# Attention and two feed-forward layers on one core: the token blocks cut as 4 x 512 + 256 instead of 512 + 4 x 448, with new planner constants

## The chip, the cores and the metric

The kernel runs on one core of a Trainium2 chip. The metric is the time of one execution in device microseconds (us); the time of a kernel is the median of its runs.

## The reference

Three steps, in float32, on 4 sequences of 576 tokens (2304 tokens in all) with 8 heads of 64:

```python
scores = q @ k.T / 8            # heads 0-3: keys at distance 0..31 back
                                # heads 4-7: keys at the same position modulo 32, not ahead
attn = softmax(scores) @ v      # -> x, 2304 x 512
xn = x / sqrt(mean(x*x) + 1e-6) * rms_g
y1 = (silu(xn @ w_gate) * (xn @ w_val)) @ w_out      # 512 -> 1536 -> 512
out = relu(y1 @ w_in)**2 @ w_out2                    # 512 -> 2048 -> 512
```

Nearly all of the arithmetic is in the two feed-forward layers: 2304 tokens through five matrices.

## The kernel before

**Attention.** There are 16 units: 4 sequences times 4 pairs of heads (two pairs of each mask). For a unit SyncE loads q, k and v, PE makes the scores, DVE takes the maximum, ACT the exponentials (`att_exp`, L414) and PE multiplies with v (`att_pv`, L502); ACT writes the result to `xr` (L536). In the first `NM2` units the mask is added by two matmuls (L354), in the others by DVE (L380).

**Feed-forward.** The tokens are cut into the blocks of the table `BLOCKS` (L49). Each layer is done in two halves of its hidden width, which makes four phases (`PHASES`): 6 + 6 tiles `j` of 128 hidden columns in layer 1, 8 + 8 in layer 2. A phase goes over the five blocks, and in a block over its tiles. So one tile of one block, a *slot*, is `ff_in` (12 matmuls, or 24 in layer 1 with gate and value) and `ff_out` (12). A matmul product is made of three passes, L1114 to L1116 (high x high, high x low, low x high parts of the operands in float32r), each with its own 128x128 weight load; a pass streams as many columns as the block has tokens, 512 or 448. On PE the order is in(j), out(j-1), in(j+1), out(j). Behind `ff_in`, `after_in` takes the sums out of PSUM: ACT makes tanh or relu (L1165, L1181), DVE gates or squares (L1169, L1177, L1185), rounds to the high part (L1194) and subtracts for the low part (L1199). Sums of `ff_out` are taken out at the end of a block (L1286, L1290, L1292).

**Weights.** They arrive as 64-bit numbers, in pairs of 128x512 tiles, and `w_task` turns each pair into high and low float32r parts: ACT or DVE takes the magnitude (L1040, L1042), DVE guards (L1049) and shifts (L1052, L1058, L1063), ACT or DVE rounds (L1072, L1074), DVE or POOL subtracts twice (L1080). The pairs live in rings of 9 and, after attention, 4 more; a pair's place comes free when the last block of its phase has used it (`through`). So the pairs of the next phase that have no place yet are made during the last block of this one.

**Norm.** `prep_task` sums the squares of runs of at most 128 tokens on PE (`chunks`, `prep_ms`), takes the inverse root on POOL, spreads it over the partitions (`prep_bc`), and DVE scales `xr` (L816). `split_tasks` makes the high part on ACT (L831) and the low part on DVE or POOL (L839).

**What sets the order.** A planner in Python walks through the program while it is built. It holds a clock for each engine, a list of tasks with due times (in slots) and a cost for each step (`dve`, `act`, `gps`, and constants such as `MXP`, `LOADF`, `TOL`), and emits the next instruction of the engine that can start first. Each engine then runs its list strictly in that order. While the planner sees PE idle before the first feed-forward matmul it puts in small matmuls on zeros (L1359). All DMAs of loads and stores stand in one list, that of SyncE (SP).

Of the kernel before, what the change touches and what calls it, by code (L numbers as in the profile page):

```python
# [16 lines left out]
B, H, S, D = 4, 8, 576, 64  # L17
# [28 lines left out]
QL, KL = {"loc": QW["loc"], "str": SL}, {"loc": KW["loc"], "str": SL}  # L46
QKW = max(QL[t] + KL[t] for t in ("loc", "str"))

BLOCKS = [(0, 512), (512, 448), (960, 448), (1408, 448), (1856, 448)]  # L49
NMAX = 512  # L50
CH = 128
NB = len(BLOCKS)
# [1 line left out]

RING, RING2 = 9, 4

ATT_LEAD, ATT_STEP = 6, 0.032
PREP_LEAD = 7.755
W_LEAD = 0.5
X_LEAD = 4.644  # L60
WARM0 = 20

HOP = 0.15
DRAIN = 0.12
TOL = 0.135
FILL, FILL_OF, T0, W1_AT = 0.113, 0.8, 5.3, 6.041
NRAW = 2
EXP = 2
QKB, SMB, TRB, PTB = 2, 3, 2, 2

NM2 = 8
QK0, PV0 = {"loc": 1.0, "str": 0.9}, {"loc": 1.25, "str": 0.9}

PRI = {"qk": -1, "mask": 1, "mx": -3, "exp": -3, "eps": -3, "sum": -1, "norm": 2, "turn": 0, "keep": 4, "tr": -3,
       "swap": 0, "pv": 9, "out": 20, "sq": 20, "ms0": 0, "add": -4}
MXP, LOADF, BIAS = 2, 0.926, 0.5

# [21 lines left out]
def chunks(i):  # L99

    out = []
    for b, s0, m in segments(*BLOCKS[i]):
        k = -(-m // CH)
        out += [(b, s0 + m - CH * (k - e)) for e in range(k)]
    return out


# [41 lines left out]
def dvx(n, fast=False):  # L149
    return [("X", (60 + n / (2 if fast else 1)) / 960 + 0.1)]  # L150


def act(n, psum=False):
    return [("A", ((172 if psum else 224) + n) / 1200 + 0.02)]


def gps(n):
    return [("P", n / 420 + 0.1)]


@with_exitstack
def kernel(ctx: ExitStack, tc: tile.TileContext, loc, strd, w1, w2, g, cst, out):
# [34 lines left out]
    ident = cst_sb[:, 0:128].bitcast(F32)  # L197
# [103 lines left out]
    first_acc, warming, ms0 = [], [True], []  # L301
# [244 lines left out]
    def att_ms0(u):  # L546

        t = ssq[0] if u == 0 else sm_t[u]
        for e, (_, s0) in enumerate(chunks(0)):
            nc.tensor.matmul(  # L550
                out=ms0[0][:CH, e:e + 1], lhsT=t[:, s0:s0 + CH], rhs=ones, start=False,
                stop=u == NPAIR - 1 and e == len(chunks(0)) - 1,
            )
# [10 lines left out]
    def att_task(u, due):  # L564
        b, p = units[u]
        kd = kind(u)
# [39 lines left out]
        def exp(i0, i1):  # L606
            def f(_, t):
                att_exp(u, i0, i1)
                if NM <= u < NM2:
                    for h in range(2):  # L610
                        if i0 < nt * (h + 1) <= i1:
                            give("s", t)
            return (None, [[("A", 0.3 * (i1 - i0) + 0.02)]], f, None, due - PRI["exp"])

        def norm(parts, t):
            att_norm(u, nc.gpsimd if parts[0][0] == "P" else nc.vector)
# [128 lines left out]
        ))  # L745
        for a in range(2):
            steps.append(step(
                "out", None, [[("A", 0.45 if kd == "loc" else 0.63)]], outp(a),
                (lambda: rel["xr"][0]) if p + a == 0 else None,
            ))  # L750
        steps.append(step(
# [5 lines left out]
        if not alone:  # L757
            m = S - add_from(b)
# [10 lines left out]
    def prep_ms(i):  # L769
        if i == 0:  # L770
            pend[0] = ms0[0], st_p.tile([128, 8], F32, tag="inv", name="inv")
            return
        ps = s_p.tile([128, 512], F32, tag="s", name="msb")
        inv = st_p.tile([128, 8], F32, tag="inv", name="inv")
        for e, (b, s0) in enumerate(chunks(i)):
            nc.tensor.matmul(out=ps[:CH, e:e + 1], lhsT=ssq[b][:, s0:s0 + CH], rhs=ones, start=True, stop=True)  # L776
        pend[i] = ps, inv

# [26 lines left out]

    def xn_parts(i, k):
# [13 lines left out]
    def split_tasks(key, due, n, src, before=None, after=None):  # L820

        cell = {"n": 0}

        def hi(k):
            def f(_, t):
                if "t" not in cell:
                    cell["t"] = x_p.tile([128, 2, KDM, NMAX], F32R, tag="x", name="xt")
                    take("x")
                    turn("x")
                for o, x in src(k):  # L830
                    nc.scalar.activation(out=cell["t"][:, 0, k, o:o + x.shape[-1]], in_=x, func=ACTF.Copy)  # L831
# [21 lines left out]
        out = []  # L853
        for k in range(KDM):
            steps = [(room_x, [act(n)], hi(k), x_time), (None, [dvx(n), gps(n)], lo(k), None)]
            out.append(Task(due, ([] if before is None else [before(k)]) + steps))
        return out

    def prep_task(i, due):
# [39 lines left out]
        def xn(k):  # L899
# [122 lines left out]
    def w_task(n, due):  # L1022
# [47 lines left out]
        def hi(parts, t):  # L1070
            if parts[0][0] == "A":
                nc.scalar.activation(out=cell["w"][:, :, 0], in_=cell["r"], func=ACTF.Copy)  # L1072
            else:
                nc.vector.tensor_copy(cell["w"][:, :, 0], cell["r"])  # L1074

        def lo(e):
            def f(parts, t):
# [397 lines left out]
```

## Time and profile before

| | |
|---|---|
| median of 3 runs | 943.73 us (940.89 to 945.85) |
| the profiled execution | 943.36 us |
| its span, first to last instruction | 941.4 us, mean granted TensorE clock 0.995 |
| PE busy, weight loads busy | 98%, 88% |
| DVE, ACT, POOL busy | 61%, 30%, 4% |
| first feed-forward matmul, last one | 50.76 us, 936.70 us after the span's start |

How to read it: the span is the profiled execution's, and some 2 us lie around it. A busy PE is not a PE at its peak, because matmuls overlap; how fast it really goes is read from the distance of the starts of its matmuls. Line numbers Lnnn are of the kernel before; the change adds two lines ahead of most of them.

### The profile page before, as it was taken

How to read it: one execution, taken by the hardware profiler on the slowest of the kernel's cores; microseconds unless marked ns; L12 is line 12 of the kernel's file. 1: busy time of each engine (PE TensorE's matmuls, PEld its weight loads, DVE VectorE, ACT ScalarE, POOL GpSimd, SP SyncE). 2: the span in 40 equal slices, each digit the busy share in tenths (PEclk: the TensorE clock that was granted, in tenths of full speed). 3: DMA queues.
4: the chain of work that ended last, by engine and by line, in shares of the span. 5: the costliest groups of instructions: out<-in, count | busy, mean ns of one | idle time of the engine just before them, and what ended most of it. 6: DMA issues, size and time to landing. Idle time of an engine off the chain costs nothing.

```text
span 941.4 us, 15656 instructions
## 1 busy us (share of the span) xinstructions
PE 927.3 (98%) x6525; PEld 829.5 (88%) x6525; DVE 576.2 (61%) x941; ACT 285.4 (30%) x773; POOL 41.0 (4%) x42
## 2 busy tenths in 40 slices
PE   8999999999999999999999999999999999999998
PEld 6777888899999888999999988999999889999997
DVE  5898856556969884243438999344459535435343
ACT  5976755523233411011112323121122211111110
POOL 0133401010000000000000000000000000000000
PEclk9999999999999999999999999999999999999999
DMA  9755654314534533030303434230221203122011
GB/s 339 236 206 182 224 170 123 113 65 183 181 132 152 178 134 123 1 118 1 123 1 128 159 138 164 99 118 1 84 76 48 79 1 123 32 87 78 1 40 39
DMA packets 47365, 105.40 MB, mean 112 GB/s; under 512 B 4160, under 2 KB 31296, under 8 KB 46272
## 3 DMA queue, kind: packets, MB, share of 16 engines
q1 hardware_dynamic: 47296, 104.41, 32.8%
q8 instruction: 51, 0.84, 0.4%
q14 instruction: 18, 0.15, 0.0%
HBM read 77.20 MB, written 23.59 MB: 107 GB/s over the span
## 4 chain that ended last, share of the span: by engine, by line
PE 94%; DMA 3%; ACT 1%; DVE 1%; issue 0%; POOL 0%; SPq 0%; DVEq 0%
PE gv L1114 18%; PE gv L1115 18%; PE gv L1116 18%; PE a L1114 12%; PE a L1115 12%; PE a L1116 12%; DMA qk<-in_loc 2%; PE xo L502 1%; PE sc L366 1%; PE a L457 1%; DMA qk<-in_strd 1%; ACT sm L414 1%; PE bc L799 0%; DMA v<-in_strd 0%; PE msb L776 0%
## 5 line engine op out<-in xcount | busy, mean ns | idle before, releaser
L1114 PE MATMUL gv<-xt,w 128*128 128x448 f32 (+1 forms) x800 | 299.2, 374 | 0.0
L1115 PE MATMUL gv<-xt,w 128*128 128x448 f32 (+1 forms) x800 | 297.0, 371 | 0.0
L1116 PE MATMUL gv<-xt,w 128*128 128x448 f32 (+1 forms) x800 | 296.8, 371 | 0.0
L1114 PE MATMUL a<-hd,w 128*128 128x448 f32 (+1 forms) x560 | 207.9, 371 | 0.0
L1115 PE MATMUL a<-hd,w 128*128 128x448 f32 (+1 forms) x560 | 207.3, 370 | 0.0
L1116 PE MATMUL a<-hd,w 128*128 128x448 f32 (+1 forms) x560 | 207.2, 370 | 0.0
L1114 PEld LDWEIGHTS gv<-xt,w 128*128 128x128 f32 x800 | 150.6, 188 | 16.6
L1115 PEld LDWEIGHTS gv<-xt,w 128*128 128x128 f32 x800 | 150.7, 188 | 16.2 <-POOL xt L839 0.4
L1116 PEld LDWEIGHTS gv<-xt,w 128*128 128x128 f32 x800 | 150.7, 188 | 15.9
L1185 DVE TENSOR_TENSOR t<-t,gv 128x448 f32<-128x448 f32 (+1 forms) x80 | 50.7, 634 | 175.9 <-ACT t L1181 175.8
L1181 ACT ACTIVATE t<-gv 128x448 f32<-128x448 f32 (+1 forms) x80 | 44.4, 555 | 303.2 <-PE gv L1116 303.1
L1114 PEld LDWEIGHTS a<-hd,w 128*128 128x128 f32 x560 | 105.2, 188 | 11.2
L1115 PEld LDWEIGHTS a<-hd,w 128*128 128x128 f32 x560 | 105.2, 188 | 11.1 <-DVE hd L1199 0.2
L1116 PEld LDWEIGHTS a<-hd,w 128*128 128x128 f32 x560 | 105.2, 188 | 11.0
L1165 ACT ACTIVATE t<-gv 128x448 f32<-128x448 f32 (+1 forms) x60 | 33.2, 553 | 209.6 <-PE gv L1116 209.4
L1169 DVE SCALAR_TENSOR_TENSOR t<-t,gv 128x448 f32<-128x448 f32 (+1 forms) x60 | 37.9, 632 | 85.0 <-ACT t L1165 84.9
L1199 DVE TENSOR_TENSOR hd<-t,hd 128x448 fp32r<-128x448 f32 (+1 forms) x136 | 86.8, 639 | 4.8 <-ACT hd L1192 0.3
L1177 DVE TENSOR_TENSOR t<-t,gv 128x448 f32<-128x448 f32 (+1 forms) x60 | 37.9, 632 | 40.5 <-PE gv L1116 39.9
L1194 DVE CAST hd<-t 128x448 fp32r<-128x448 f32 (+1 forms) x132 | 52.8, 400 | 9.3
L1040 ACT ACTIVATE raw<-wst 128x1024 f32<-128x1024 f32 x24 | 27.3, 1142 | 40.6 <-DMA wst<-in_w 33.3
L414 ACT ACTIVATE sm<-sm,nm 128x64 f32<-128x64 f32 x88 | 29.3, 335 | 17.6 <-DVE nm L402 17.5
L839 DVE TENSOR_TENSOR xt<-xs,xt 128x448 fp32r<-128x448 f32 (+1 forms) x60 | 34.3, 632 | 0.0
(86 smaller groups left out, 673.2 us busy)
## 6 DMA issues: line engine op xcount, KB each, us to landing
wst<-in_w SPq DMA_DIRECT2D x34, 1024.0 KB, 5.0
yp_d<-ys SPq DMA_DIRECT2D x8, 896.0 KB, 4.3
ypt<-yp_d SPq DMA_DIRECT2D x8, 896.0 KB, 7.9
xs<-y_d SPq DMA_DIRECT2D x8, 896.0 KB, 5.1
qk<-in_strd SPq DMA_DIRECT2D x8, 604.0 KB, 6.4
qk<-in_loc SPq DMA_DIRECT2D x8, 592.0 KB, 6.0
xs<-xn_d SPq DMA_DIRECT2D x4, 896.0 KB, 5.5
y_d<-ys SPq DMA_DIRECT2D x4, 896.0 KB, 4.8
```

The lines of the kernel that those rows point to most:

```text
L414: nc.scalar.activation(out=sm[:, i], in_=sm[:, i] if sc is None else sc[h][:, 64 * t:64 * t + 64], func=ACTF.Exp, bias=nm[:, i:i + 1], sca ...
L839: eng.tensor_tensor(out=cell["t"][:, 1, k, c], in0=x, in1=cell["t"][:, 0, k, c].bitcast(F32), op=ALU.subtract)
L1114: nc.tensor.matmul(out=o, lhsT=whi, rhs=x_hi, start=first, stop=False)
L1115: nc.tensor.matmul(out=o, lhsT=whi, rhs=x_lo, start=False, stop=False)
L1116: nc.tensor.matmul(out=o, lhsT=wlo, rhs=x_hi, start=False, stop=last)
L1165: nc.scalar.activation(out=tile_t()[:, :n], in_=ps[:, :n], func=ACTF.Tanh, scale=0.5)
L1169: nc.vector.scalar_tensor_tensor(out=t_sb[:, :n], in0=t_sb[:, :n], scalar=1.0, in1=ps[:, :n], op0=ALU.add, op1=ALU.mult)
L1177: nc.vector.tensor_tensor(out=t_sb[:, :n], in0=t_sb[:, :n], in1=ps[:, :n], op=ALU.mult)
L1181: nc.scalar.activation(out=tile_t()[:, :n], in_=ps[:, :n], func=ACTF.Relu)
L1185: nc.vector.tensor_tensor(out=t_sb[:, :n], in0=t_sb[:, :n], in1=ps[:, :n], op=ALU.mult)
L1194: nc.vector.tensor_copy(hid[key][0][:, 0, :n], tmps[key][:, :n])
L1199: eng.tensor_tensor(out=hd[:, 1, :n], in0=t_sb[:, :n], in1=hd[:, 0, :n].bitcast(F32), op=ALU.subtract)
```

## The change

`BLOCKS` becomes four blocks of 512 tokens and a last one of 256. The number of slots and of matmuls in the feed-forward layers stays as it is. Because block ends now fall at other places of the sequences, `chunks` names for each run its first token in the sequence, how many of 128 to skip, and its length, and `prep_bc` uses these. The planner gets other leads, priorities and costs, and the masks of a ninth unit are added by PE.

```diff
-BLOCKS = [(0, 512), (512, 448), (960, 448), (1408, 448), (1856, 448)]
+BLOCKS = [(0, 512), (512, 512), (1024, 512), (1536, 512), (2048, 256)]
...
-ATT_LEAD, ATT_STEP = 6, 0.032
-PREP_LEAD = 7.755
-W_LEAD = 0.5
-X_LEAD = 4.644
+ATT_LEAD, ATT_STEP = 7, 0
+PREP_LEAD = 2.463
+W_LEAD = 2.25
+X_LEAD = 3.773
...
-TOL = 0.135
-FILL, FILL_OF, T0, W1_AT = 0.113, 0.8, 5.3, 6.041
+TOL = 0.215
+FILL, FILL_OF, T0, W1_AT = 0.113, 0.8, 5.3, 9.414
...
-NM2 = 8
+NM2 = 9
...
-MXP, LOADF, BIAS = 2, 0.926, 0.5
+MXP, LOADF, BIAS = 16, 0, 0.729
-PV_AHEAD = 3
+PV_AHEAD = 2
...
     for b, s0, m in segments(*BLOCKS[i]):
-        k = -(-m // CH)
-        out += [(b, s0 + m - CH * (k - e)) for e in range(k)]
+        for o in range(0, m, CH):
+            c = min(CH, m - o)
+            first = min(s0 + o, S - CH)
+            out.append((b, first, s0 + o - first, c))
...
 def gps(n):
-    return [("P", n / 420 + 0.1)]
+    return [("P", n / 400 + 0.18)]
...
-        for e, (b, s0) in enumerate(chunks(i)):
-            skip = CH * len(chunks(i)) - BLOCKS[i][1] if e == 0 else 0
+        for e, (_, _, skip, m) in enumerate(chunks(i)):
             nc.tensor.matmul(
-                out=ps[:, o:o + CH - skip], lhsT=inv[:CH, e:e + 1].to_broadcast([CH, 128]), rhs=ident[:CH, skip:CH],
+                out=ps[:, o:o + m], lhsT=inv[:CH, e:e + 1].to_broadcast([CH, 128]), rhs=ident[:CH, skip:skip + m],
                 start=True, stop=True,
             )
-            o += CH - skip
+            o += m
```

Left out: the table `PRI` of priorities (nearly every entry is another) and five costs of ACT and PE steps.

**What moves: SyncE's list at the start.** The sixth to tenth transfers of the program (`wst` is a pair of raw weights, `qk` and `v` are a unit's inputs). Before:

```order
L329 DMA v<-in_strd 128x768
L996 DMA wst<-in_w 128x2x1024
L321 DMA qk<-in_loc 128x1184
L323 DMA qk<-in_strd 128x2x604
L996 DMA wst<-in_w 128x2x1024
```

With the change:

```order
L331 DMA v<-in_strd 128x768
L323 DMA qk<-in_loc 128x1184
L325 DMA qk<-in_strd 128x2x604
L998 DMA wst<-in_w 128x2x1024 x2
L323 DMA qk<-in_loc 128x1184
```

The second pair of weights now stands behind the q and k of units 2 and 3, and directly ahead of the third pair.

**DVE ahead of the first feed-forward matmul.** (`xr` is the attention output, `xt` the block's split operand, `w` a pair's split parts.) Before:

```order
L428 RECIPROCAL ri<-su 128x10
L435 TENSOR_TENSOR sm<-sm,ri 128x640
L1063 SCALAR_TENSOR_TENSOR raws<-wst,raws 128x1024
L816 SCALAR_TENSOR_TENSOR xr<-xr,g_sb,bc 128x512 x4
L839 TENSOR_TENSOR xt<-xr,xt 128x512 x3
```

With the change:

```order
L430 RECIPROCAL ri<-su 128x10
L437 TENSOR_TENSOR sm<-sm,ri 128x640
L1076 CAST w<-raws 128x2x512
L817 SCALAR_TENSOR_TENSOR xr<-xr,g_sb,bc 128x512 x4
L840 TENSOR_TENSOR xt<-xr,xt 128x512 x4
```

All four low parts of the first block are now DVE's; one of them was POOL's. In this list up to the low parts there are one rounding and one subtraction of weights more than before.

**DVE in the last block of phase 0, its first two slots.** Before (448 tokens):

```order
L1169 SCALAR_TENSOR_TENSOR t<-t,gv 128x448
L1177 TENSOR_TENSOR t<-t,gv 128x448
L1194 CAST hd<-t 128x448
L1199 TENSOR_TENSOR hd<-t,hd 128x448
L1049 TENSOR_SCALAR raw<-raw 128x1024
L1052 TENSOR_SCALAR raw<-raw 128x1024
L1292 TENSOR_SCALAR ys<-a_3313 128x448
L1058 SCALAR_TENSOR_TENSOR raw<-wst,raw 128x1024
L1063 SCALAR_TENSOR_TENSOR raw<-wst,raw 128x1024
L1169 SCALAR_TENSOR_TENSOR t<-t,gv 128x448
```

With the change (256 tokens):

```order
L1171 SCALAR_TENSOR_TENSOR t<-t,gv 128x256
L1179 TENSOR_TENSOR t<-t,gv 128x256
L1196 CAST hd<-t 128x256
L1201 TENSOR_TENSOR hd<-t,hd 128x256
L1051 TENSOR_SCALAR raw<-raw 128x1024
L1054 TENSOR_SCALAR raw<-raw 128x1024
L1060 SCALAR_TENSOR_TENSOR raw<-wst,raw 128x1024
L1294 TENSOR_SCALAR ys<-a_3333 128x512
L1065 SCALAR_TENSOR_TENSOR raw<-wst,raw 128x1024
L1171 SCALAR_TENSOR_TENSOR t<-t,gv 128x256
```

The same operations stand there; those of the block are 256 wide, those of the weights as wide as before. From the first gate (L1171) of this block to its last low part (L1201) the list holds, beside the block's own operations, three each of L1051, L1054, L1060 and L1065, four of L1082 (subtraction of weights) and one eviction (L1294).

## Rows read from the trace of the kernel before

**Rows 1.** The page, busy time by engine.
```profile
PE 927.3 (98%) x6525; PEld 829.5 (88%) x6525; DVE 576.2 (61%) x941; ACT 285.4 (30%) x773; POOL 41.0 (4%) x42
```
**Rows 2.** Groups of instructions by line: busy us, mean ns of one | idle before.
```profile
L1114 PE MATMUL gv<-xt,w 128*128 128x448 f32 (+1 forms) x800 | 299.2, 374 | 0.0
...
L1114 PE MATMUL a<-hd,w 128*128 128x448 f32 (+1 forms) x560 | 207.9, 371 | 0.0
...
L1114 PEld LDWEIGHTS gv<-xt,w 128*128 128x128 f32 x800 | 150.6, 188 | 16.6
```
**Rows 3.** Stretches: length, busy PE PEld DVE ACT POOL, granted clock, DMA share, GB/s.
```profile
50.70:115.30 64.60, 64.07 (x829) 51.35 (x819) 56.11 (x83) 46.98 (x176) 24.10 (x22) 1.00 0.61 206
115.30:176.70 61.40, 59.49 (x838) 52.12 (x837) 36.87 (x69) 36.93 (x156) 3.68 (x4) 0.97 0.45 134
...
270.30:314.40 44.10, 44.10 (x218) 40.60 (x217) 38.82 (x57) 17.18 (x23) 0.00 (x0) 1.00 0.42 138
314.40:362.80 48.40, 48.40 (x218) 40.53 (x217) 39.56 (x58) 13.33 (x19) 0.00 (x0) 1.00 0.42 147
```
**Rows 4.** Timeline of PE, a block of 512: starts of two slots four slots apart.
```profile
322.44 0.39 PE L1114 MATMUL gv<-xt,w 128*128 128x512 f32 x1
...
355.08 0.39 PE L1114 MATMUL gv<-xt,w 128*128 128x512 f32 x1
```
**Rows 5.** The same, a block of 448.
```profile
414.34 0.36 PE L1114 MATMUL gv<-xt,w 128*128 128x448 f32 x1
...
443.52 0.36 PE L1114 MATMUL gv<-xt,w 128*128 128x448 f32 x1
```
**Rows 6.** Timeline of PE: eight loads with one column each; zeros of 256 columns, two windows.
```profile
98.02 0.95 PE L776 MATMUL msb<-ones,ssq 128*128 128x1 f32 x8
...
8.19 3.54 PE L1359 MATMUL warm<-blank 128*128 128x256 bf16 x30
...
8.19 2.98 PE L1359 MATMUL warm<-blank 128*128 128x256 bf16 x25
```
**Rows 7.** Groups by form: DVE and ACT operations of a block.
```profile
L1199 DVE TENSOR_TENSOR hd<-t,hd 128x448 fp32r<-128x448 f32 x110 | 68.8, 626 | 4.0 <-ACT hd L1192 0.3
L1194 DVE CAST hd<-t 128x448 fp32r<-128x448 f32 x110 | 43.4, 394 | 7.6
L1169 DVE SCALAR_TENSOR_TENSOR t<-t,gv 128x448 f32<-128x448 f32 x48 | 29.7, 619 | 79.0 <-ACT t L1165 79.0
L1199 DVE TENSOR_TENSOR hd<-t,hd 128x512 fp32r<-128x512 f32 x26 | 18.0, 692 | 0.8
...
L1181 ACT ACTIVATE t<-gv 128x448 f32<-128x448 f32 x64 | 34.8, 544 | 245.4 <-PE gv L1116 245.3
```
**Rows 8.** Groups by form: DVE operations of a pair of weights.
```profile
L1080 DVE TENSOR_TENSOR w<-raw,w 128x512 fp32r<-128x512 f32 x49 | 32.1, 686 | 1.3 <-ACT w L1072 1.0
L1058 DVE SCALAR_TENSOR_TENSOR raw<-wst,raw 128x1024 int32<-128x1024 int32 x25 | 30.6, 1223 | 0.5
```
**Rows 9.** Timeline, the start: when unit 2 and the second weights came.
```profile
16.52 1.13 ACT L1040 ACTIVATE raws<-wst 128x1024 f32<-128x1024 f32 x1 [0.34 <-DMA wst<-in_w]
...
18.06 0.71 PE L366 MATMUL a<-qk 64*32 64x64 f32 x46 [0.92 <-DMA qk<-in_loc]
...
20.20 0.82 DVE L397 TENSOR_REDUCE nm<-a 128x10 f32<-128x640 f32 x1 [1.38 <-PE a L366]
```
**Rows 10.** Timeline, the first feed-forward matmuls and the low parts they wait for.
```profile
49.27 4.23 DVE L839 TENSOR_TENSOR xt<-xr,xt 128x512 fp32r<-128x512 f32 x3
...
51.30 0.19 PEld L1115 LDWEIGHTS gv<-xt,w 128*128 128x128 f32 x1 [0.35 <-POOL xt L839]
```
**Rows 11.** Timeline of PE, the longest wait in phase 0 and matmuls behind it.
```profile
145.91 1.04 PE L502 MATMUL xo<-pt,v 64*64 64x64 f32 x44 [1.91 <-DMA v<-in_strd]
...
147.69 0.58 PE L1114 MATMUL gv<-xt,w 128*128 128x448 f32 x1
...
150.31 0.58 PE L1115 MATMUL gv<-xt,w 128*128 128x448 f32 x1
```

More of the change, by code (lines that the diff above doesn't have):

```diff
@@ L69 @@
 QKB, SMB, TRB, PTB = 2, 3, 2, 2
-NM2 = 8
+NM2 = 9
 QK0, PV0 = {"loc": 1.0, "str": 0.9}, {"loc": 1.25, "str": 0.9}
-PRI = {"qk": -1, "mask": 1, "mx": -3, "exp": -3, "eps": -3, "sum": -1, "norm": 2, "turn": 0, "keep": 4, "tr": -3,
-       "swap": 0, "pv": 9, "out": 20, "sq": 20, "ms0": 0, "add": -4}
-MXP, LOADF, BIAS = 2, 0.926, 0.5
-D_BUSY, D_COST = 120, 1.1
-PV_AHEAD = 3
+PRI = {"qk": 1, "mask": 0, "mx": -1, "exp": 0, "eps": 0, "sum": 0, "norm": 2, "turn": -5, "keep": 0, "tr": 0,
+       "swap": -1, "pv": 0, "out": 0, "sq": -3, "ms0": -3, "add": -3}
+MXP, LOADF, BIAS = 16, 0, 0.729
+D_BUSY, D_COST = 121.519, 1.1
+PV_AHEAD = 2
 NM = 6
@@ L548, in att_ms0 @@
         t = ssq[0] if u == 0 else sm_t[u]
-        for e, (_, s0) in enumerate(chunks(0)):
+        for e, (_, s0, _, _) in enumerate(chunks(0)):
             nc.tensor.matmul(
@@ L612, in f @@
                             give("s", t)
-            return (None, [[("A", 0.3 * (i1 - i0) + 0.02)]], f, None, due - PRI["exp"])
+            return (None, [[("A", 0.33 * (i1 - i0))]], f, None, due - PRI["exp"])
         def norm(parts, t):
@@ L747, in att_task @@
             steps.append(step(
-                "out", None, [[("A", 0.45 if kd == "loc" else 0.63)]], outp(a),
+                "out", None, [[("A", 0.47 if kd == "loc" else 0.73)]], outp(a),
                 (lambda: rel["xr"][0]) if p + a == 0 else None,
@@ L774, in prep_ms @@
         inv = st_p.tile([128, 8], F32, tag="inv", name="inv")
-        for e, (b, s0) in enumerate(chunks(i)):
+        for e, (b, s0, _, _) in enumerate(chunks(i)):
             nc.tensor.matmul(out=ps[:CH, e:e + 1], lhsT=ssq[b][:, s0:s0 + CH], rhs=ones, start=True, stop=True)
@@ L796, in prep_bc @@
         o = 0
-        for e, (b, s0) in enumerate(chunks(i)):
-            skip = CH * len(chunks(i)) - BLOCKS[i][1] if e == 0 else 0
+        for e, (_, _, skip, m) in enumerate(chunks(i)):
             nc.tensor.matmul(
-                out=ps[:, o:o + CH - skip], lhsT=inv[:CH, e:e + 1].to_broadcast([CH, 128]), rhs=ident[:CH, skip:CH],
+                out=ps[:, o:o + m], lhsT=inv[:CH, e:e + 1].to_broadcast([CH, 128]), rhs=ident[:CH, skip:skip + m],
                 start=True, stop=True,
             )
-            o += CH - skip
+            o += m
         pend[i] = ps, inv
@@ L853, in split_tasks @@
         out = []
+        two = 0.23 * (len(list(src(0))) - 1)
         for k in range(KDM):
-            steps = [(room_x, [act(n)], hi(k), x_time), (None, [dvx(n), gps(n)], lo(k), None)]
+            steps = [(room_x, [[("A", act(n)[0][1] + two)]], hi(k), x_time), (None, [dvx(n), gps(n)], lo(k), None)]
             out.append(Task(due, ([] if before is None else [before(k)]) + steps))
@@ L927, in prep_task @@
             (None, [[("P", 1.1)]], pw, None),
-            (lambda: room("s"), [[("T", 0.4 * nch)]], bc, lambda: rel["s"][0]),
+            (lambda: room("s"), [[("T", 0.25 * nch)]], bc, lambda: rel["s"][0]),
         ]))
@@ L1089, in w_task @@
                 and (keys[0][0] == 0 or "raw" in late),
-                [dvx(1024, fast=True), act(1024)], size,
+                [dvx(1024, fast=True), [("A", 1.14)]], size,
                 lambda: max(
```

## The prediction

> **What bounds the kernel now.** I read the page first: PE is busy for 98% of the span, no other engine for two thirds [rows 1]. A busy PE may still be a slow one, so the next view is the timeline of PE, for the distance between the starts of its matmuls. In a block of 512 tokens two slots that are four slots apart start at 322.44 and 355.08 us [rows 4]. A slot of layer 1 has 36 matmuls, so 32.64 us / 144 = 226.7 ns each. In a block of 448 it is 29.18 us / 144 = 202.6 ns [rows 5]. The granted clock is 1.00 there, the level of 2.4 GHz [rows 3], at which 512 columns take 213.3 ns and 448 take 186.7. So a matmul costs its columns plus 13.4 ns at 512, but plus 15.9 ns at 448. Then the table of stretches: after 226 us PE never rests, in a block with heavy weight work as little as elsewhere [rows 3]. What is not such streaming lies in front: 50.7 us until the first feed-forward matmul, attention's own matmuls in phase 0, and a few waits there. DVE is the engine to watch: at the two ends of phase 0 and 1 it works 38.8 of 44.1 us, and 39.6 of the 48.4 us of the block behind [rows 3].
>
> **Streaming, the first term.** The feed-forward layers have 3 x (800 + 560) = 4080 passes [rows 2], 816 to a block. Their number stays and so does the sum of columns. Only the widths move: per pass of each block, 4 x 226.7 + x takes the place of 226.7 + 4 x 202.6, where x is the distance at 256 columns with a new 128x128 load each time. That is x - 130.5 ns, times 816. No row of before shows x. From below: 256 columns of zeros in bf16 with a load each run at (3.54 - 2.98) us / 5 = 112 ns [rows 6]; x = 112 gives -15.1 us. From above: a straight line through 448 and 512 (24.1 ns for 64 columns) gives x = 130.5, and no gain at all. Between them, 106.7 ns of columns plus what is paid at 512 gives 120, plus what is paid at 448 gives 122.6. I take 120, because 512 is the nearer kind: 256 is its half, while 448, no such multiple, pays more. 816 x (120 - 130.5) = **-8.6 us** (-6.5 by 448's rest).
>
> **Waits in the narrow block, the second term.** In layer 2 a slot of 256 has 24 passes, 2.88 us. From the end of in(j) to out(j) lie 24 passes, in which ACT and DVE must make the operand: at 448 that is 0.54 + 0.62 + 0.39 + 0.63 = 2.18 us; 192 columns fewer save up to 0.2 us each (626 against 692 ns for 64 columns), so some 1.4 to 1.6 us [rows 7]. The rest, 1.3 us, is as long as one weight operation of 1.22 us that stands in between on DVE [rows 8], with handovers not counted. In the very last slot only 12 passes, 1.44 us, cover the chain: a wait of a few tenths, against a last eviction that is 0.2 us shorter. In layer 1 the cover is 36 passes of 120 ns, 4.3 us. In phase 0's last block DVE has 6 x (0.42 + 0.42 + 0.3 + 0.43) = 9.4 us of its own and, by the list, eleven shorter operations taken at 0.69 and six at 1.22, 14.9 us [rows 7, 8]: 24.3 of 25.9 us. It fits, barely. I take **+1 us**, with 0 and +6 as ends.
>
> **The start, the third term.** Unit 2's scores waited 0.92 us for its DMA at 18.06, and DVE 1.38 us for those scores at 20.20 [rows 9]. With the second weights (1 MB) behind units 2 and 3, that wait should go. What is late next is the second weights themselves: ACT took them at 16.52 [rows 9], and its list still has them ahead of unit 0's output and unit 2's exponentials, so ACT now waits for two more transfers of 0.6 MB, and everything queued behind it too. DVE does 1.4 us more (a rounding and a subtraction at 0.69, [rows 8]) before it scales the first block; against that its three low parts took 4.23 us beside POOL, where three alone take 2.1 at 0.69, and PE waited 0.35 us for POOL's [rows 7, 10]. With DVE making all four, that goes. -1.4 + 1.4 - 0.7, and a little from POOL: **-1 us**, ends -4 and +3.
>
> **The rest of phase 0, the fourth term.** PE lost 1.9 us idle to a late v at 145.91, and then ran eight matmuls at 374 ns ((150.31 - 147.69) / 7, the level of 1.2 GHz after that idle time) in place of 203, 1.4 us more [rows 11]; 0.5 us idle in the block before [rows 3]. All order here is new, so each wait may go or another come. Wider blocks give each sequence's attention some 5 us more to finish in, hence **-1.5 us**, ends -3.8 and +4. The mask of the ninth unit adds two matmuls, at most 0.23 us each at a full 512 [rows 4]: **+0.5 us** (DVE is relieved). `chunks` makes 16 runs as before: nothing; a run of norm done late shows in the term just given. The DMAs of a block grow from 896 KB to 1 MB with a longer block to hide them.
>
> Sum: -8.6 + 1 - 1 - 1.5 + 0.5 = -9.6 us, on the profiled execution's 943.4 us: **933.8 us**. That execution lies 0.04% under the median, so nothing is corrected for it.
>
> **Rivals.** *L, the straight line:* x is 130 and the streaming term is zero. For it: it is the only line through the two measured widths. Against: it makes a 256 pass pay 24 ns beside its columns, more than either. 933.8 + 8.6 = 942.4 us. The Trainium skill's page "TensorE: Matmul & The Clock Gate", section "Back-to-back issue gap", gives the distance as N / 2.4 plus a fixed 2.5 ns at the high clock; with number and sum of columns unchanged that rule, too, makes the streaming term zero. The trace does not agree with one fixed cost: the rest is 13.4 at 512 and 15.9 at 448.
>
> *D, DVE becomes the bound at the narrow block (slower).* The work beside the block's own is not narrower, the time for it is: before, 38.8 us of DVE less 6 x (0.62 + 0.62 + 0.39 + 0.63) = 13.5 leaves 25.3 us [rows 3, 7]; with 9.4 that is 34.7 us in 25.9, 8.8 too many at each end of a layer-1 phase. The next block has just 8.8 us of DVE free [rows 3]. If the order lets none of that be used (the weights are needed in turn), PE waits 8.8 us twice, with 1.4 us at the low clock behind each: 933.8 + 20.4 = 954 us. It decides from 4.8 us per end on. Against: the list holds only 14.9 us there, the rest has been moved to wide blocks.
>
> *W, weight loads bind.* A load's record is 188 ns long [rows 2]; if loads follow each other, x = 188, 816 x 57.5 = +46.9 us, some 988 us with the other terms but the waits. Against: eight loads with one column each took 0.95 us, at most 119 ns each [rows 6], so records overlap. The Trainium skill's page "Perfetto Trace Analysis", section "Identifying the Most-Contended Engine", takes the busy share of LDWEIGHTS as the measure of TensorE's headroom; by it the 88% here would leave little, and a block where the records fill more than its time would be bound by loads, as W says. The overlap in the last rows speaks against that reading.
>
> **Numbers.** Forecast 0.70, L 0.16, D 0.11, W 0.03. A measurement of this kernel can tell about 0.5% (4.7 us) from no change: under 939 is faster, over 948.4 slower. Of the forecast 0.04 ends within (waits at their upper ends), of L 0.02 is faster; of D 0.07 is slower, 0.04 within (half the wait); W is slower. Faster 0.68, same 0.22, slower 0.10. The range goes down by x = 112 alone, 933.8 - 6.5 = 927, and up past L to 946, where D is half priced; out of it are W, most of D and the tails, about 0.2.
>
> **What would show it.** Slots of layer 1 in the 512 blocks every 8.16 us, in the 256 block every 4.3 us (4.7 by L, 6.8 by W); in its timeline passes 120 ns apart without gaps, DVE near 95% busy. Gaps at the start of phases 1 and 2 with waits for `w` on DVE would be D. First feed-forward matmul near 50 us; ACT waiting for `wst` near 17 us if the third term's counterweight is real. Block starts after phase 0 should come 49.0 us apart in layer 1 and 43.5 in layer 2, the narrow one 25.9 and 23.0 long. Wrong would make it: x above 126, several us of DVE-ended gaps in layer 2's narrow blocks, or a late load that stops PE long enough to halve its clock more than once.

## The result, and the profile after

The changed kernel takes 934.95 us (median of 16 executions, 929.86 to 938.47) against 943.27 us (16 executions, 939.18 to 945.85). The ratio is 0.9906, with the interval 0.9891 to 0.992. Its profiled execution took 935.57 us with a span of 933.8 us; the profiled one of before 943.36 and 941.4. So the two profiles stand 7.65 us apart (933.79 against 941.44 us of span), the medians 8.3 us. Line numbers of the changed kernel are those of before plus two; the three passes are L1116, L1117 and L1118.

The page, busy time by engine, and the granted clock in 40 slices (a digit of 9 is 90% or more):

```profile
PE 924.2 (99%) x6539; PEld 779.8 (84%) x6539; DVE 581.7 (62%) x956; ACT 285.5 (31%) x775; POOL 23.3 (2%) x25
...
PEclk9799999999999999999999999999999999999999
```

Beside [rows 1] PE is as full as before, DVE and ACT do as much, and POOL does a little over half. Only in the second slice, 23 to 47 us, does the clock fall below nine tenths on average.

**Streaming.** Timeline of PE: two passes 144 passes apart, in a block of 512 and in the narrow block of 256:

```profile
323.30 0.39 PE L1116 MATMUL a<-hd,w 128*128 128x512 f32 x1
...
355.94 0.39 PE L1116 MATMUL a<-hd,w 128*128 128x512 f32 x1
...
514.03 0.28 PE L1116 MATMUL a<-hd,w 128*128 128x256 f32 x1
...
531.31 0.28 PE L1116 MATMUL a<-hd,w 128*128 128x256 f32 x1
```

At 512 it is 32.64 us / 144 = 226.7 ns, as in [rows 4]; at 256 it is 17.28 us / 144 = 120.0 ns. So x is 120, and the streaming term 816 x (120 - 130.5) = -8.6 us, as predicted.

**The narrow block and phase 0.** Stretches of the changed kernel (columns as in [rows 3]): nearly the first two blocks of phase 0, and its narrow one from its first matmul to the next block's:

```profile
55.40:118.80 63.40, 63.40 (x784) 51.59 (x777) 56.51 (x87) 42.43 (x147) 13.24 (x11) 1.00 0.62 208
118.80:182.60 63.80, 63.80 (x885) 51.25 (x883) 40.52 (x73) 36.14 (x155) 1.01 (x1) 1.00 0.46 137
...
283.72:310.93 27.21, 27.21 (x217) 26.72 (x216) 24.48 (x45) 11.56 (x18) 0.00 (x0) 1.00 0.46 160
```

PE no longer rests in the second block, and its clock is 1.00 there, where [rows 3] has 59.49 of 61.40 us at 0.97. In the narrow block DVE works 24.5 of 27.2 us and PE still never waits. The largest gaps that PE has in or behind narrow blocks are two in layer 2, at the start of its first phase and in the last slot of all (timeline of PE):

```profile
539.68 0.39 PE L1116 MATMUL a<-hd,w 128*128 128x512 f32 x1
540.25 0.50 PE L1117 MATMUL a<-hd,w 128*128 128x512 f32 x1 [0.18 <-DVE hd L1201]
...
927.68 0.39 PE L1116 MATMUL a<-hd,w 128*128 128x256 f32 x1
928.14 0.38 PE L1117 MATMUL a<-hd,w 128*128 128x256 f32 x1
```

The starts are 0.57 and 0.46 us apart in place of 0.23 and 0.12: 0.7 us in all.

**The start.** The first feed-forward matmul comes at 55.42 us, not at 50.76. Two stretches, in the kernel before:

```profile
20.00:24.00 4.00, 4.00 (x71) 3.87 (x59) 3.66 (x6) 1.40 (x8) 0.00 (x0) 0.65 1.00 303
36.00:52.00 16.00, 14.78 (x347) 12.20 (x347) 13.80 (x22) 15.06 (x58) 4.74 (x4) 1.00 0.82 282
```

and in the changed one:

```profile
36.00:52.00 16.00, 16.00 (x218) 14.13 (x219) 9.73 (x19) 9.95 (x49) 3.32 (x3) 0.57 0.69 241
20.00:24.00 4.00, 4.00 (x72) 3.66 (x68) 3.31 (x4) 2.74 (x12) 0.00 (x0) 0.59 0.87 287
```

From 20 to 24 us both run at a low clock. From 36 to 52 us the changed kernel alone does: the mean is 0.57, which is nearly all of the stretch at 1.2 GHz, and PE gets through 218 matmuls where before it did 347. Its timeline shows what PE did ahead of that:

```profile
33.10 0.74 PE L368 MATMUL a<-qk 64*32 64x64 f32 x51
35.14 0.45 PE L368 MATMUL a<-qk 64*32 64x64 f32 x29 [1.30 <-issue]
35.52 1.05 PE L552 MATMUL ms<-ones,sq 128*128 128x1 f32 x8
36.50 2.50 PE L459 MATMUL a<-cst_sb,sm 64*64 64x64 f32 x48
...
55.42 0.50 PE L1116 MATMUL gv<-xt,w 128*128 128x512 f32 x1
...
237.48 0.39 PE L1116 MATMUL gv<-xt,w 128*128 128x512 f32 x1
```

In the middle of the fifth unit's 80 scores PE stood still for 1.3 us ("issue": nothing that the profile shows held it). Behind that come eight matmuls of one column, and then the 48 matmuls of the turn (`att_turn`, which transposes the exponentials) take 2.50 us. Before, they took 1.61, after a stop just as long; there the turn stood right behind the scores, and the eight matmuls of one column behind the turn:

```profile
36.34 0.45 PE L366 MATMUL a<-qk 64*32 64x64 f32 x29 [1.33 <-issue]
36.72 1.61 PE L457 MATMUL a<-cst_sb,sm 64*64 64x64 f32 x48
...
226.69 0.36 PE L1114 MATMUL gv<-xt,w 128*128 128x448 f32 x1
```

The last rows of the two fences are the thirteenth matmul of phase 0's fourth block: 182.06 us after the first matmul with the change, 175.93 before. Up to there 432 passes are 64 columns wider, which explains 432 x 24.1 ns = 10.4 us of the difference, so the rest of phase 0 gained 4.3 us. Attention has not moved across the border: both kernels have the same numbers of its scores, turns and products with v (464, 216 and 232 matmuls) ahead of the first feed-forward matmul.

The wait for the second weights is there as well (waits of the changed kernel, 0 to 56 us: engine, line, releaser, us in total, times, longest):

```profile
ACT raws L1042 <- DMA wst<-in_w: 3.3, 1, 3.3
...
DVE xr L817 <- PE bc L800: 1.6, 1, 1.6
DVE inv L784 <- PE ms L552: 1.6, 1, 1.6
```

The other two lines are waits for PE's slow matmuls, right ahead of the first block. So the account is -8.6 (streaming) + 0.8 (gaps of PE from the fourth block on, 1.2 us where before had 0.35) + 4.7 (start) - 4.3 (rest of phase 0) - 0.3 (a shorter end behind the last matmul) = -7.7 of -7.65 us.

### The profile page after: what moved, and what is told of

Same layout as the page of the kernel before. It is cut to its first block, busy times and chain, and to the rows that moved or that the text cites. A ratio compares the mean times of both kernels' runs of the same rounds, so it can differ in the third digit from the quotient of the medians.

```text
span 933.8 us, 15670 instructions
## 1 busy us (share of the span) xinstructions
PE 924.2 (99%) x6539; PEld 779.8 (84%) x6539; DVE 581.7 (62%) x956; ACT 285.5 (31%) x775; POOL 23.3 (2%) x25
## 4 chain that ended last, share of the span: by engine, by line
PE 96%; DVE 2%; DMA 1%; issue 1%; SPq 0%; ACT 0%; DVEq 0%
PE gv L1116 18%; PE gv L1118 17%; PE gv L1117 17%; PE a L1116 12%; PE a L1117 12%; PE a L1118 12%; PE xo L504 2%; PE a L459 1%; PE warm L1361 1%; PE sc L368 1%; DMA wst<-in_w 1%; PE ms L552 1%; PE bc L800 1%; PE a L368 0%; PE msb L778 0%
## 5 line engine op out<-in xcount | busy, mean ns | idle before, releaser
L1116 PE MATMUL gv<-xt,w 128*128 128x512 f32 (+1 forms) x800 | 296.9, 371 | 0.0
L1117 PE MATMUL gv<-xt,w 128*128 128x512 f32 (+1 forms) x800 | 294.5, 368 | 0.0
L1118 PE MATMUL gv<-xt,w 128*128 128x512 f32 (+1 forms) x800 | 294.5, 368 | 0.0
L1116 PE MATMUL a<-hd,w 128*128 128x512 f32 (+1 forms) x560 | 206.9, 369 | 0.0
L1117 PE MATMUL a<-hd,w 128*128 128x512 f32 (+1 forms) x560 | 206.4, 368 | 0.3 <-DVE hd L1201 0.2
L1118 PE MATMUL a<-hd,w 128*128 128x512 f32 (+1 forms) x560 | 206.0, 368 | 0.0
L1116 PEld LDWEIGHTS gv<-xt,w 128*128 128x128 f32 x800 | 150.8, 189 | 25.4
L1118 PEld LDWEIGHTS gv<-xt,w 128*128 128x128 f32 x800 | 150.8, 188 | 25.4
L1117 PEld LDWEIGHTS gv<-xt,w 128*128 128x128 f32 x800 | 150.9, 189 | 24.4
L1187 DVE TENSOR_TENSOR t<-t,gv 128x512 f32<-128x512 f32 (+1 forms) x80 | 50.6, 633 | 161.3 <-ACT t L1183 161.2
L1183 ACT ACTIVATE t<-gv 128x512 f32<-128x512 f32 (+1 forms) x80 | 44.4, 555 | 293.1 <-PE gv L1118 290.6
L1117 PEld LDWEIGHTS a<-hd,w 128*128 128x128 f32 x560 | 105.6, 189 | 18.1 <-DVE hd L1201 0.9
L1116 PEld LDWEIGHTS a<-hd,w 128*128 128x128 f32 x560 | 105.6, 189 | 17.8
L1118 PEld LDWEIGHTS a<-hd,w 128*128 128x128 f32 x560 | 105.6, 189 | 17.6
L1167 ACT ACTIVATE t<-gv 128x512 f32<-128x512 f32 (+1 forms) x60 | 33.3, 555 | 205.1 <-PE gv L1118 205.1
L1171 DVE SCALAR_TENSOR_TENSOR t<-t,gv 128x512 f32<-128x512 f32 (+1 forms) x60 | 37.9, 631 | 87.8 <-ACT t L1167 87.7
L1201 DVE TENSOR_TENSOR hd<-t,hd 128x512 fp32r<-128x512 f32 (+1 forms) x139 | 89.2, 641 | 5.2 <-ACT hd L1194 0.7
L1179 DVE TENSOR_TENSOR t<-t,gv 128x512 f32<-128x512 f32 (+1 forms) x60 | 38.0, 634 | 41.1 <-PE gv L1118 40.4
L1196 DVE CAST hd<-t 128x512 fp32r<-128x512 f32 (+1 forms) x131 | 52.2, 399 | 9.9 <-DVE t L1187 0.9
L1082 DVE TENSOR_TENSOR w<-raw,w 128x512 fp32r<-128x512 f32 x50 | 32.9, 687 | 2.2 <-ACT w L1074 2.0
L832 ACT ACTIVATE xt<-xs 128x512 fp32r<-128x512 f32 (+1 forms) x60 | 30.3, 579 | 11.9 <-PE gv L1118 11.9
```

Of the source, the lines that this page charges most:

```text
L1082: eng.tensor_tensor(out=w[:, 1], in0=cell["r"][:, e], in1=w[:, 0].bitcast(F32), op=ALU.subtract)
L1116: nc.tensor.matmul(out=o, lhsT=whi, rhs=x_hi, start=first, stop=False)
L1117: nc.tensor.matmul(out=o, lhsT=whi, rhs=x_lo, start=False, stop=False)
L1118: nc.tensor.matmul(out=o, lhsT=wlo, rhs=x_hi, start=False, stop=last)
L1167: nc.scalar.activation(out=tile_t()[:, :n], in_=ps[:, :n], func=ACTF.Tanh, scale=0.5)
L1171: nc.vector.scalar_tensor_tensor(out=t_sb[:, :n], in0=t_sb[:, :n], scalar=1.0, in1=ps[:, :n], op0=ALU.add, op1=ALU.mult)
```

## The experiments

Two questions were left: does the streaming gain stand by itself, and what made the start late? **Theory C**: the low clock that followed PE's stop. **Rival A**: the second weights, for which ACT waits 3.3 us. The table has each kernel's median beside its ratio to before on the same chip. The fourth column counts the executions whose granted clock, averaged over the span, was 0.997 or more, and the last gives the first feed-forward matmul in the profiled one. The kernel before had 18 of 56 such executions. In every profile the clock is 1.00 from 60 to 925 us, but for 0.91 behind the late v in the kernel before (140 to 160 us). Of executions without a profile only the mean is on record, so that they too lost their clock in the start is inferred.

| kernel | us | ratio, interval | clock >= 0.997 | first matmul |
|---|---|---|---|---|
| changed, 16 executions | 934.95 | 0.9906, 0.9891 to 0.992 | 2 of 16 | 55.42 |
| changed, once more | 932.45 | 0.9897, 0.987 to 0.9924 | 1 of 6 | 54.16 |
| new blocks alone | 938.00 | 0.9945, 0.9925 to 0.9965 | 5 of 11 | 49.75 |
| new planner alone | 941.44 | 0.998, 0.996 to 0.9999 | 1 of 12 | 50.04 |
| second weights early | 933.85 | 0.991, 0.9879 to 0.994 | 1 of 6 | 51.82 |
| fills ahead | 930.61 | 0.9872, 0.9842 to 0.9902 | 5 of 6 | 49.05 |
| fills behind | 931.77 | 0.9884, 0.9855 to 0.9913 | 5 of 6 | 51.71 |
| fills at two units | 931.81 | 0.987, 0.9844 to 0.9896 | 6 of 6 | 51.54 |
| fills ahead and behind | 931.42 | 0.9891, 0.9859 to 0.9923 | 5 of 6 | 50.84 |
| no fills | 940.67 | 0.9968, 0.9948 to 0.9988 | 0 of 10 | 58.78 |
| before, with fills | 941.88 | 0.9991, 0.9971 to 1.0011 | 7 of 12 | 50.62 |

### New blocks alone

The new `BLOCKS`, `chunks` and `prep_bc` with all constants, priorities and costs of before.

```diff
-ATT_LEAD, ATT_STEP = 7, 0
+ATT_LEAD, ATT_STEP = 6, 0.032
...
-FILL, FILL_OF, T0, W1_AT = 0.113, 0.8, 5.3, 9.414
+FILL, FILL_OF, T0, W1_AT = 0.113, 0.8, 5.3, 6.041
```

> The new blocks (with the new runs of norm, which they need) under the planner constants of before. Theory S (the streaming distance makes the gain, whatever the planner): passes of 256 columns 120 ns apart, as in the changed kernel, so 816 x (120 - 130.5) = -8.6 us; the first feed-forward matmul near 50.8 us as before; waits of phase 0 and of the narrow blocks within 3 us of before either way. 943.3 - 8.6 = 934.7 us, 932 to 938. Rival P (the wide gain needs the new planner, because the old one leaves too much of DVE's weight work beside the narrow block): gaps that DVE ends at the beginning of phases 1 and 2, 2 to 9 us each, and 939 us or more.

Measured: 0.9945 and 938.0 us, the upper end of theory S. Passes of 256 are 120.0 ns apart here too, and the start is not late. Timeline of PE, the first feed-forward matmul and the fourth block's thirteenth, then the waits of PE between 234 and 320 us:

```profile
49.75 0.50 PE L1116 MATMUL gv<-xt,w 128*128 128x512 f32 x1
...
234.76 0.39 PE L1116 MATMUL gv<-xt,w 128*128 128x512 f32 x1
```

```profile
PE gv L1116 <- DVE t L1171: 1.1, 2, 0.8
```

Phase 0 up to that matmul takes 185.0 us here, some 3 more than in the changed kernel, and in the fourth block and the narrow one behind it PE waits 1.1 us for DVE's gate. That is rival P in its manner, but not in its size, and not at the beginning of phases 1 and 2. By the medians the blocks alone give 4.8 us of the 8.3, although this profile has the streaming term in full; the new planner takes away those waits and some 3 us of phase 0. What the other ten executions lost beside the profiled one (934.62 us) no trace shows.

### New planner alone

```diff
-BLOCKS = [(0, 512), (512, 512), (1024, 512), (1536, 512), (2048, 256)]
+BLOCKS = [(0, 512), (512, 448), (960, 448), (1408, 448), (1856, 448)]
```

> The new planner constants with the blocks of before (512 and four of 448). Theory S: no pass of 256, so the streaming term is gone; what is left is the planner's own: the start 4.7 us later (first feed-forward matmul near 55.4 us) and phase 0 without its late v, 3 to 4 us less: 943 to 945 us. Rival P (the planner makes the gain): 938 us or less. If the 4 us that phase 0 gained came with the wider blocks, not with the planner: 947 to 949 us.

Timeline of PE, the same two matmuls:

```profile
50.04 0.50 PE L1116 MATMUL gv<-xt,w 128*128 128x512 f32 x1
...
221.65 0.37 PE L1116 MATMUL gv<-xt,w 128*128 128x448 f32 x1
```

That is 171.6 us against 175.9 before, in the same blocks: the 4.3 us of phase 0 are the planner's, and no wait of PE is listed there. Yet the median falls by only 1.4 us, to a time that none of the three expectations had. The profiled execution had a clock of 0.998, but the other eleven had less, down to 0.990. That most of them lost in the start what phase 0 gained is inferred from these means; they have no trace.

### Fills ahead of the fifth unit

Here and below, `zeros[0]` is the planner's own `fill`, which issues matmuls of 256 columns on zeros.

```diff
     def att_qk(u):
...
         nt = tiles(u)
+        if u == 4:
+            zeros[0](12)
         masked = u < NM2
```

> The changed kernel with 12 more matmuls on zeros on PE ahead of the masks of the fifth unit, near 32.6 us. Theory C (the start is late because PE ran at the low clock from about 36.5 to 50 us after it had stood still for 1.3 us in the fifth unit's scores, with few matmuls on zeros around them): the granted clock stays at 1.00 there, the first feed-forward matmul comes at 55.4 - 6 + up to 1.3 = 49.5 to 51 us, and the time falls by 4 to 6 us, to 929 to 931 us, with the mean clock of every run at 0.997 or more. Rival A (it is late because ACT waited 3.3 us for the second weights, and the clock only follows): the fills add their 1.3 us or hide, the first feed-forward matmul stays at 54 to 57 us, 934 to 937 us.

Timeline of PE, and below it the stretch of 36 to 52 us:

```profile
33.67 1.04 PE L370 MATMUL a<-qk 64*32 64x64 f32 x80
...
49.05 0.50 PE L1118 MATMUL gv<-xt,w 128*128 128x512 f32 x1
```

```profile
36.00:52.00 16.00, 15.73 (x326) 13.35 (x321) 15.11 (x27) 15.11 (x61) 3.52 (x3) 1.00 0.85 298
```

The 80 scores run through in 1.04 us with no stop, the clock is 1.00, and the first matmul comes 6.4 us earlier although 1.3 us of fills were added. One of six executions still had 0.994. ACT's wait for the second weights is still there, and longer, so rival A falls:

```profile
ACT raws L1044 <- DMA wst<-in_w: 3.9, 1, 3.9
```

### Second weights early

```diff
-FILL, FILL_OF, T0, W1_AT = 0.113, 0.8, 5.3, 9.414
+FILL, FILL_OF, T0, W1_AT = 0.113, 0.8, 5.3, 6.041
```

> The changed kernel with the second pair of weights loaded ahead of the q and k of the third and fourth unit again (one constant). Theory A (the late weights make the start late): ACT's wait of 3.3 us at 19.4 goes, the first feed-forward matmul comes 2 to 4 us earlier, 51.5 to 53.5 us, and the time falls to 931 to 933 us. Theory C (the clock makes it late): the weights are not on the way that ends last, the third unit's scores wait some 1 us again as before; if PE still runs at the low clock from about 36 us, the first feed-forward matmul stays at 54 us or later and the time at 934 to 937 us.

Timeline of ACT, and of PE:

```profile
16.84 1.11 ACT L1042 ACTIVATE raws<-wst 128x1024 f32<-128x1024 f32 x1
```

```profile
17.99 1.04 PE L368 MATMUL a<-qk 64*32 64x64 f32 x80 [1.28 <-DMA qk<-in_loc]
```

ACT's wait is gone, and PE's wait for the third unit's q and k is back, 1.28 us where [rows 9] had 0.92. The median, 933.85 us, lies between the two expected ranges, and the ratio is that of the changed kernel. The first matmul at 51.82 lies where rival A had it, but this execution had its clock at 1.00 from 36 us on and lost it from 20 to 28 us instead, so it does not speak for A. The two orders of these transfers are one wait against another.

### Fills behind the fifth unit

The run with fills ahead took away both the stop and the thin work after it. Here the fills follow the scores.

```diff
         for h in range(2):
             s_ps[u, h] = sc[h]
+        if u == 4:
+            zeros[0](12)
```

> The same 12 matmuls on zeros as in the run with them ahead of the fifth unit's masks, but right behind that unit's scores. The run ahead had taken away two things at once: PE's stop of 1.3 us within those scores and the sparse stretch after it. Theory C1 (the stop brings the low clock, whatever follows): the stop of 1.3 us within the 80 scores is still there, most executions still lose clock in the start (means of 0.989 to 0.996), 934 to 936 us. Theory C2 (the few columns that PE streams around it bring it): the stop is there, the clock holds, as with the fills ahead: 930 to 932 us.

Timeline of PE:

```profile
35.68 0.45 PE L368 MATMUL a<-qk 64*32 64x64 f32 x29 [1.14 <-issue]
36.06 1.52 PE L1363 MATMUL warm<-blank 128*128 128x256 bf16 x12
...
38.29 1.61 PE L461 MATMUL a<-cst_sb,sm 64*64 64x64 f32 x48
```

The stop is there, 1.14 us, and the turn behind it takes 1.61 us all the same, the time of the high level. So the stop alone does not bring the low clock, which rules out C1 and fits C2. What in the thin work behind it does bring it, this run does not separate.

### Fills at two units

```diff
     def att_pv(u):
+        if u == 0:
+            zeros[0](12)
```

This in addition to the fills ahead of the fifth unit.

> The changed kernel with 12 matmuls on zeros ahead of the fifth unit's masks and 12 more ahead of the first unit's product with v, near 16.5 us, where PE stood still for 1.9 us (put down to issue) within that product. If slower matmuls ahead of a long row of short ones take such a stop away, as ahead of the fifth unit's scores, the stop of 1.9 us shrinks to under 0.5, the first feed-forward matmul comes at 48 to 49.5 us, and every run's mean clock is at 0.998 or more: 929 to 930 us, with a narrower spread than 929.0 to 934.2. If the stop there is the late transfer or another thing, the 1.2 us of fills are added ahead of it: 930.5 to 932 us.

Timeline of PE:

```profile
16.53 1.51 PE L1365 MATMUL warm<-blank 128*128 128x256 bf16 x12
17.97 0.55 PE L508 MATMUL xo<-pt,v 64*64 64x32 f32 x24
19.20 0.90 PE L508 MATMUL xo<-pt,v 64*64 64x32 f32 x48 [0.68 <-issue]
...
40.91 0.80 PE L508 MATMUL xo<-pt,v 64*64 64x64 f32 x35 [1.11 <-issue]
```

The stop at the first unit shrank from 1.9 to 0.68 us, but others appeared, 0.82 us in the fifth unit's scores and 1.11 us at 40.91. The stops moved with the length of PE's list more than they went away. All six executions kept their clock, but the first matmul comes at 51.54 us, not at 48 to 49.5, and the time is no lower than with the fills ahead alone.

### No fills

The 20 fills at the very start stay; the planner's 100 others are gone.

```diff
-FILL, FILL_OF, T0, W1_AT = 0.113, 0.8, 5.3, 9.414
+FILL, FILL_OF, T0, W1_AT = 0.113, 0.0, 5.3, 9.414
```

> The changed kernel without the 100 matmuls on zeros that the planner puts in after the first 20. Theory C (the clock in the start is what costs): PE runs at the low level for most of the stretch from 15 to 50 us, about twice as long as the 18 us in the profile of the changed kernel, so the first feed-forward matmul comes at 57 to 63 us and the time is 938 to 944 us. Rival A (other waits set the start): 53 to 56 us, 932 to 936 us, since the fills are not there to be run either.

```profile
36.00:52.00 16.00, 15.25 (x318) 13.83 (x318) 10.32 (x19) 11.21 (x44) 0.21 (x1) 0.56 0.56 171
```

The stretch is as slow as the changed kernel's, and from 16 to 28 us the clock is 0.50 throughout. The first matmul comes at 58.78 us, the mean clock is 0.975 to 0.984, and the ratio 0.9968 lies clear of the changed kernel's. C holds, with the size it gave.

### Fills ahead and behind, with the changed kernel beside it

> The changed kernel once more, on the same chip as the kernel with fills that stands beside it, so that the two can be compared directly. Every theory: 933 to 937 us, mean clocks of 0.989 to 0.999 from execution to execution, as in its 16 executions so far.

> The changed kernel with 12 matmuls on zeros ahead of the fifth unit's masks and 12 more behind its scores. Theory C2 (the sparse stretch of PE around these scores brings the low clock): the clock holds from 33 us on, first feed-forward matmul at 49 to 52 us, 930 to 932 us, and against the changed kernel beside it 3 to 5 us less. Rival (the fills ahead gained by taking the stop of 1.3 us away, and the 12 behind now only cost their 1.3 us): 932 to 934 us, the clock no better than with the fills ahead alone.

The stretch of 36 to 52 us in the changed kernel's second profile:

```profile
36.00:52.00 16.00, 16.00 (x215) 13.99 (x212) 9.97 (x18) 10.70 (x50) 3.50 (x3) 0.58 0.65 235
```

The low clock is in the same place again, here after a stop of 0.75 us. But against each other the two medians differ by 1.0 us, not by 3 to 5, and the intervals overlap; the changed kernel's own median was 0.55 us under the expected range. What the clock does is plain: 21 of the 24 executions with some form of these fills had 0.997 or more, and 3 of the changed kernel's 22. What it is worth in the median is not: 931.6 us over those 24 against 933.4 us over these 22, from different chips.

### The kernel before with the same fills

> The kernel before, with the same 12 matmuls on zeros ahead of the fifth unit's masks. If the kernel before loses clock there as often as the changed one, it gains as much, 3 to 4 us, to 939 to 940 us, and the fills belong to no part of the change. If it keeps its clock there in most executions (it had 12 matmuls on zeros more between the fourth unit's and the fifth's work), it gains 0 to 1.5 us at most, 941 to 943 us, and the change itself made the start more sensitive.

0.9991, not to be told from no change. But this does not show that the fills belong to the changed order. On this chip the fills lower the median by 1.4 us here (943.30 to 941.88) and by 1.0 us in the changed kernel, neither clear of noise, and 7 of 12 executions reach 0.997 here where 4 of 17 do without fills. Nor is the kernel before shown to lose clock there less often: 18 of its 56 executions reach 0.997 against 3 of 22, and some of its loss lies in phase 0, behind the late v. From 28 to 32 us the profile of before has 12 matmuls on zeros where that of the changed kernel has 6, which is six more and not 12.

### Other widths

Two runs with other blocks, for the distance of passes. First 512, 480, 416, 384 and 512 tokens, then 512, 512, 496, 464 and 320.

> The changed kernel with blocks of 512, 480, 416, 384 and 512 tokens, for the distance of passes at other widths. Theory L (a straight line through 448 and 512): 214.7 ns at 480, 190.6 at 416, 178.6 at 384. Theory E (each width pays its columns and 13.3 ns, and 448 is an exception): 213.3, 186.7 and 173.3. Theory M (multiples of 128 pay 13.3 ns, other widths 15.9): 215.9, 189.2 and 173.3. The time is not compared; its sum of columns is that of the changed kernel, so by E it is within 1 us of it in streaming, by M 960 passes pay 2.6 ns more, 2.5 us.

> The changed kernel with blocks of 512, 512, 496, 464 and 320 tokens. So far a pass pays its columns and 13.4 to 13.6 ns at 256, 384, 416 and 512, but 16.0 at 448 and 16.7 at 480 (there by turns 221 and 212 ns). If what is paid rises only between 416 and 512: 320 pays 13.4 (146.7 to 146.9 ns), 464 some 16.4 (209.7), 496 between 13.5 and 17 (220.2 to 223.7). If it hangs on how a width divides (416 by 32, 448 by 64), 496 and 464, which are multiples of 16 alone, pay alike.

Timeline of PE, passes 144 apart, in the first of them at 480 and 416:

```profile
367.15 0.37 PE L1116 MATMUL a<-hd,w 128*128 128x480 f32 x1
...
398.35 0.37 PE L1116 MATMUL a<-hd,w 128*128 128x480 f32 x1
...
412.51 0.35 PE L1116 MATMUL a<-hd,w 128*128 128x416 f32 x1
...
439.39 0.35 PE L1116 MATMUL a<-hd,w 128*128 128x416 f32 x1
```

and in the second at 496:

```profile
416.70 0.38 PE L1116 MATMUL a<-hd,w 128*128 128x496 f32 x1
...
448.38 0.38 PE L1116 MATMUL a<-hd,w 128*128 128x496 f32 x1
```

| columns | 256 | 320 | 384 | 416 | 448 | 464 | 480 | 496 | 512 |
|---|---|---|---|---|---|---|---|---|---|
| ns from pass to pass | 120.0 | 146.7 | 173.3 | 186.7 | 202.6 | 210.0 | 216.7 | 220.0 | 226.7 |
| beside the columns at 2.4 GHz | 13.3 | 13.3 | 13.3 | 13.3 | 15.9 | 16.7 | 16.7 | 13.3 | 13.3 |

None of the rules that were written down holds throughout: not the line, not the multiples of 128 (416, 320 and 496 pay the lesser price), not the rise up to 512 (496). What holds is that 448 to 480 pay 2.6 to 3.3 ns more than every other width tried. At 480 the passes come by turns after 221 and 212 ns; but so they do after 215 and 205 ns at 464 and after 189 and 184 at 416, which pays the lesser price. Why these widths, no run here shows. The two kernels took 933.25 and 933.03 us (one execution each).

The first of these two runs also settles what the clock costs the start. Up to the first feed-forward matmul its PE has the very list of the changed kernel, 1088 matmuls with no fills added:

```profile
34.62 0.45 PE L368 MATMUL a<-qk 64*32 64x64 f32 x29 [1.15 <-issue]
...
49.92 0.50 PE L1116 MATMUL gv<-xt,w 128*128 128x512 f32 x1
```

```profile
36.00:52.00 16.00, 15.40 (x327) 13.11 (x327) 14.75 (x28) 14.63 (x62) 3.52 (x3) 1.00 0.79 285
```

The stop is there, the clock stays at 1.00, and the first matmul comes at 49.92 us: 5.5 us earlier than in the changed kernel's profile, with the same work on PE. So with this list the clock falls in some executions and not in others; the list alone does not decide it.

## Why the prediction was right, and where it was not

The time, 933.8 us against a median of 934.95, was right, and the main term with it. That the sum came so near is partly luck: one term had the wrong sign, 5.7 us off, and another's surplus of 3.3 us made up for more than half of it.

- **The streaming term held exactly**: x = 120.0 ns, -8.6 us. Blocks of layer 1 begin 48.96 us apart (358.66 to 407.62), those of layer 2 43.52 (575.52 to 619.04), as foretold. Its reason was only half right. The prediction chose 120 because 256 is half of 512 and 448 "no such multiple". But 320, 416 and 496 are no such multiples either and pay the same 13.3 ns. The exception is 448, and the whole streaming gain is leaving it: 4 blocks x 816 passes x 2.6 ns = 8.5 us.
- **The waits of the narrow block** were taken at +1 us and measured +0.8. In phase 0 the prediction counted 24.3 us of work for DVE in 25.9 us and found that it barely fits; it was 24.5 of 27.2 us, with no wait. The block is 1.3 us longer than foretold because its first 12 `ff_out` passes still belong to the block ahead and are 512 wide; that is no loss, as the block behind is shorter by as much. Rival D is out: under the old constants, too, PE waited only 1.1 us for the gate, in the narrow block and the one ahead of it.
- **The start failed.** The step that failed is the third term, -1 us; measured was +4.66. Its items were right: the third unit's scores no longer wait, ACT waits 3.28 us for the second weights, up to 19.42 us, and DVE makes all four low parts in 2.5 us, where three took 4.2. Where the clock held, its size was right too: in the first run of other widths the first feed-forward matmul comes at 49.92 us, which is -0.84. But no duration in that sum is one of PE at the low clock. The prediction reckoned with a halved clock only behind a late load in phase 0; of the start it uses no stretch (those of [rows 3] begin at 50.7 us), and it has no term for what the profile then showed, 16 us at a clock of 0.57 behind the fifth unit's scores; with the shorter low stretch near 20 us that cost 5.5 us. Why some executions lose their clock there and others with the same list do not, stays open.
- **The rest of phase 0** was taken at -1.5 and +0.5 us and gave -4.3. All of the 1.9, 1.4 and 0.5 us that the prediction named went, together its lower end of -3.8. Why it is 0.5 us more, and why the 0.5 us for the ninth unit's mask does not show, no row says. The new planner in the old blocks shows the same 4.3 us, so it came from the order, not from the wider blocks.
- **Rival L** is out by x. The Trainium skill's page "TensorE: Matmul & The Clock Gate", section "Back-to-back issue gap", gives the isolated distance as N / 2.4 and one fixed cost per matmul; here that cost is 13.3 ns at six widths and 15.9 to 16.7 ns at three, so the measurement decides against it, and a rule with one fixed cost would have seen no gain.
- **Rival W** is out: in the narrow block weight loads fill 26.72 of 27.21 us by their records, and the passes still come every 120 ns. The Trainium skill's page "Perfetto Trace Analysis", section "Identifying the Most-Contended Engine", judges TensorE's headroom by MFU and by that busy share. The trace does not agree on the share: it is 98% in the narrow block and 84% over the span, while columns at 2.4 GHz fill 89% of a pass of 256 and 94% of one of 512.

## What to carry to other kernels

Measure the distance of matmul starts at each width that the kernel uses: two kernels with the same number of passes and columns can differ by 0.9% because one width pays 2.6 ns more a pass. When a change reorders work ahead of the steady part, read PE's granted clock there in short stretches, and for several executions, before costing it by rows at the high level. A few matmuls on zeros where PE's work is thin are cheap: 12 of them are 1.3 us of PE, and with 12 or 24 the mean clock was 0.997 or more in 21 of 24 executions. Their gain in the median, 1.0 us beside the changed kernel on one chip, is not clear of noise.

## What the runs showed of the hardware

- One kernel's executions differ with their mean clock, and in the profiles the loss lies in the first 60 us. The changed kernel's spans run from 928.1 us (mean clock 0.999) to 936.7 us (0.989): 8.6 us, as much as the change is worth. The Trainium skill's page "TensorE: Matmul & The Clock Gate", section "Part 1: The HAM clock gate", says that the clock follows how busy PE has lately been and that the loss varies from run to run. The traces agree on the variation: from 36 to 52 us the same list of PE had 0.57 in one execution and 1.00 in another.
- PE stops for 0.5 to 2.1 us in the middle of long rows of matmuls of some 15 ns each, put down to issue. With 12 slower matmuls ahead of one such row its stop of 1.3 us went away; with 12 more ahead of another row, stops came at other places. What PE waits for there stays open.
- The extra 2.6 to 3.3 ns a pass at 448, 464 and 480 columns, and the uneven turns at 416, 464 and 480, stay unexplained.
